# Constant matmuls on TensorE in the first units and before the fp32 job; units through the eleventh's routing ahead of the third job

## The chip, the cores and the metric

The kernel runs on one core of a Trainium2 chip. The metric is the device time of one launch in microseconds (us), as a median of several runs. The engines are named as the profile names them: PE is TensorE (PEld its weight loads), DVE is VectorE, ACT is ScalarE, POOL is GpSimd, SP is SyncE, which here only issues DMAs.

## What is computed

A gated scan over 4 sequences of 3648 tokens of 256 values, and then a mixture of 16 experts in 4 groups of 4. Each token goes to the best group and, in it, to the best expert; its row is multiplied by that expert's two matrices (256 x 1024 and 1024 x 256) and by the two softmax weights.

```python
f = lower_bound + (1.0 - lower_bound) * sigmoid(f_logit);  i = 1.0 - f
for t in range(S):
    h = f[:, t] * h + i[:, t] * x[:, t];  y[:, t] = h
x = y.reshape(B * S, D)                      # 14592 rows of 256
g_idx = argmax(x @ w_group, axis=1)
e_idx = argmax(xg @ w_expert[g], axis=1)     # rows of group g
out[tok_idx] = g_w * e_w * (maximum(x_e @ w1[g, e], 0.0) @ w2[g, e])
```

## The kernel before

**Units.** The 14592 tokens are cut into 29 units of 512. A unit's data is loaded into a tile `zt` by one DMA (line 179). ACT forms the gate (tanh in line 189, an affine step of two pieces in line 199); DVE multiplies (line 215 or 235, one instruction of 1024 columns) and scans (line 226, two instructions of 512 columns into `h`). PE transposes `h` back to rows (line 253, eight 128-column transposes per unit; ACT copies them in line 255) and forms router logits (line 267; ACT copies `rs` in line 270; PE turns them in line 278; ACT copies `Lg` in line 279).

**Routing.** Units are routed in groups, mostly of two. DVE finds the best group and expert (lines 288 to 306), PE counts with the constant matrices `tri`, `upto` and `ones` (lines 313 and 314, in the first nine units lines 368 to 371), DVE makes positions (`both` in line 336 up to `posi` in line 344) and weights (lines 320 to 330). POOL then scatters each block of 128 rows to its expert's list `xs` in HBM (line 348, eight scatters per group of two units).

**Jobs.** Sixteen early jobs, one per expert, each start as soon as a given unit (the cut) has been routed: cut 7 for the first two, 9 for the third and fourth, 11 for the fifth and sixth, and so on. They take 256 rows or more. Sixteen later jobs do the rest. A job's rows `xr` are loaded from `xs` by SP (line 805), and transposed on PE (line 885). Its weights come in four pieces `st` of 512 KB (line 823); ACT makes the upper half `wh` (line 831) and DVE the lower half `wl` (line 832). The first product is three matmuls per block (lines 938 to 940), evicted by ACT as `hh` (line 943) and by DVE as `hl` (line 944); the second product is line 968. One chunk of 256 rows is 48 matmuls of each product. The very first job runs in fp32 without halves (lines 916 and 951); the text calls it the fp32 job. The fourth job is the one that follows the third; "the fifth job's rows" are those of the first job with cut 11.

**Order.** Each engine works strictly through its own list. In the last part of the function a loop goes over the jobs; between their matmuls `bg_step` takes steps from `bgq`, the list of unit and routing steps, at a rate that has them done when a later job is due. `start_macro` first runs `bg_to(marks[cut])`, which empties `bgq` to the point at which the next job's rows are asked for. The program's scheduler then fixes the order on each engine from this sequence, and it can shift instructions against each other. PSUM tiles come from `bank`: three buffers for `m1`, two for `m2`, three for `p`.

Of the kernel before, what the change touches and what calls it, by code (L numbers as in the profile page):

```python
# [18 lines left out]
P = 128  # L19
NE = 16  # L20
UNIT = 512
# [24 lines left out]
def gated_scan_moe(ctx: ExitStack, tc, zx, lower, wroute, wexp, out, S):  # L46
    nc = tc.nc
# [27 lines left out]
    def bank(tag):  # L75
        return ps.tile([P, UNIT], F32, name=f"ps_{tag}", tag=tag, bufs=PS_BUFS[tag])
# [49 lines left out]
    tri = const.tile([P, P], BF16, name="tri")  # L126
    nc.gpsimd.tensor_scalar(out=tri, in0=dmat, scalar1=0.0, scalar2=None, op0=ALU.is_gt)
    upto = const.tile([P, P], BF16, name="upto")
# [109 lines left out]
    def p1_back(u, i):  # L238
# [17 lines left out]
        if i == 0:  # L256
            nc.scalar.copy(rows.bitcast(I32)[:, 0:nt, D], tokno[:, a // P:a // P + nt])

    def p1_router(u):
        a, b = unit_range(u)  # L260
        nt = (b - a) // P
        h = units[u]["h"]
        rp = bank("p")
        for k in range(KD):
            for j in range(nt):
                q = 32 * j
                nc.tensor.matmul(rp[q:q + 32, 0:P], wr[:, k, :], h[:, k, j * P:(j + 1) * P],
                                 start=(k == 0), stop=(k == KD - 1), tile_position=(0, q))
        rs = p1.tile([P, P], F32, name="rs")
        nc.scalar.copy(rs[0:32 * nt], rp[0:32 * nt, 0:P])  # L270
        units[u]["rs"] = rs
# [9 lines left out]
    def route_thunks(G, T, fast=False):  # L281
# [80 lines left out]

        def f4():
            pp = R["pp"] = bank("p")
            oh16 = R["oh16"]
            pv = pp[:, 0:(T + 1) * NE].rearrange("p (t e) -> p t e", e=NE)
            run = state["runoff"][0:1, None, :].broadcast_to([1, T + 1, NE])
            nc.tensor.matmul(pv, row1, run, start=True, stop=False)
            nc.tensor.matmul(pv[:, 0:T], upto, oh16, start=False, stop=False)
            for t in range(T):  # L370
                nc.tensor.matmul(pv[:, t + 1:T + 1], ones, oh16[:, t:t + 1, :].broadcast_to([P, T - t, NE]),
                                 start=False, stop=(t == T - 1))
# [461 lines left out]
    def job_xt(j, pi):  # L834
        b0, rows = j.pieces[pi]
        ch = max(i for i, (a, _) in enumerate(j.chunks) if a <= b0)
        c0 = b0 - j.chunks[ch][0]
        if j.raw:
            j.xh[ch] = mo.tile([P, 2 * P], F32, name="xh", bufs=X_BUFS)
            j.xl[ch] = mo.tile([P, 2 * P], F32, name="xl", bufs=X_BUFS)  # L840
        elif c0 == 0:
            j.xh[ch] = mo.tile([P, KD, 2 * P], F16, name="xh", bufs=X_BUFS)
            j.xl[ch] = mo.tile([P, KD, 2 * P], BF16, name="xl", bufs=X_BUFS)
# [183 lines left out]
    def bg_to(n):  # L1027
        while done[0] < n:
            bg_pop()
# [80 lines left out]
    for mi, mac in enumerate(macros):  # L1110
        if mi < len(PLAN):
            continue
        q = deque()
        if mi + 1 < len(macros):
            start_macro(mi + 1)
            for j in macros[mi + 1]:
                q.extend(prep_thunks(j))
        left = work(mac)
        for j in mac:
            for ch in range(len(j.chunks)):  # L1120
                for cs in j.cols[ch]:
                    m1_step(j, ch, cs)
                    left -= len(cs)
                    bg_step(q, left - 2, len(cs))
                if pending is not None:
                    pj, pc = pending
                    for t in range(len(pj.parts[pc])):
                        m2_step(pj, pc, t)
                        left -= 1
                        bg_step(q, left - 2, 1)  # L1130
                    if pc == len(pj.chunks) - 1:
                        live[0] -= 1
                pending = (j, ch)
        while q:
            q.popleft()()
# [66 lines left out]
```

## Time and profile before

| | us |
|---|---|
| median of three runs (774.38 to 777.86) | 775.78 |
| the profiled execution | 776.59 |
| its span, first to last instruction | 774.8 |
| PE busy in the span | 716.6 (92%) |
| DVE busy | 533.9 (69%) |
| ACT busy | 458.8 (59%) |

Times within the profile count from the span's start; 1.8 us lie outside it. The page gives busy time by engine, the other views used below are tables of stretches (busy time of each engine and the clock that TensorE was granted, 1.00 for 2.4 GHz and 0.50 for 1.2 GHz), lists of who waited for whom, and instructions of one engine in order of time. An entry in square brackets at the end of a row is the idle time before the instruction and what ended it.

### The profile page before, as it was taken

The page shows a single profiled execution, that of the slowest core. Times are in us where ns is not written, and L with a number is a line of the kernel's source. Part 1 is how long each engine was busy: PE and PEld are TensorE (multiplying, and loading weights), DVE is VectorE, ACT ScalarE, POOL GpSimd, SP SyncE. Part 2 cuts the span into 40 slices and gives each one's busy share as a digit, 9 for nine tenths or more (in the row PEclk, how much of TensorE's full clock was granted, in tenths as well). Part 3 has the DMA queues.
Part 4 walks back from the last instruction along what each step waited for, and adds up shares of the span by engine and source line. Part 5 has one row for each costly group of instructions (what it writes and reads, how often), then busy time and mean ns, then how long its engine had stood idle before and what let it go on. Part 6 is the DMA issues. An engine that isn't in the chain of part 4 may idle for free.

```text
span 774.8 us, 20906 instructions
## 1 busy us (share of the span) xinstructions
PE 716.6 (92%) x8055; PEld 633.7 (82%) x8055; DVE 533.9 (69%) x1046; ACT 458.8 (59%) x822; POOL 286.6 (37%) x272
## 2 busy tenths in 40 slices
PE   2656996989999999999999999999999999999995
PEld 1434885778888888889888898999999999999995
DVE  6898798898999976786465545555564676666640
ACT  6586785867878955455455444454555465555541
POOL 3663248276556543642111122213222322232222
PEclk9985998999999999999999999999999999999998
DMA  7998898889998845588656343553553556555300
GB/s 278 352 376 301 306 303 246 320 281 314 317 326 287 266 152 124 171 223 203 170 133 135 120 101 108 134 127 120 139 168 101 158 158 173 158 168 175 88 30 24
DMA packets 104037, 151.75 MB, mean 196 GB/s; under 512 B 63938, under 2 KB 73952, under 8 KB 100608
## 3 DMA queue, kind: packets, MB, share of 16 engines
q1 hardware_dynamic: 89248, 102.00, 45.3%
q0 software_dynamic: 11424, 30.02, 10.8%
q10 hardware_dynamic: 3264, 18.39, 6.9%
q8 instruction: 63, 1.03, 0.6%
q14 instruction: 38, 0.31, 0.1%
HBM read 112.69 MB, written 38.19 MB: 195 GB/s over the span
## 4 chain that ended last, share of the span: by engine, by line
PE 63%; DVE 11%; issue 10%; DMA 10%; POOL 4%; ACT 1%; SPq 0%; POOLq 0%; DVEq 0%; ACTq 0%
PE ps_m L968 29%; PE ps_m L938 7%; PE ps_m L939 7%; PE ps_m L940 7%; DMA xs<-rows,posi 4%; DMA zt<-in_zx_dram 3%; PE ps_p L938 3%; PE ps_p L940 3%; PE ps_p L939 3%; POOL out_dram L981 3%; DVE h L226 2%; DVE wl L832 2%; DMA xr<-xs 2%; PE ps_p L253 1%; DVE hl L944 1%
## 5 line engine op out<-in xcount | busy, mean ns | idle before, releaser
L968 PE MATMUL ps_m<-wh,hl 128*128 128x256 f16 (+4 forms) x1304 | 261.4, 251 | 0.0
L968 PE MATMUL ps_m<-wl,hh 128*128 128x256 bf16 (+4 forms) x1304 | 261.2, 250 | 0.1
L968 PE MATMUL ps_m<-wh,hh 128*128 128x256 f16 (+4 forms) x1304 | 261.1, 251 | 0.0
L968 PEld LDWEIGHTS <-hh 128*128 128x128 f16 (+2 forms) x2608 | 192.3, 99 | 23.4 <-issue 3.7
L938 PE MATMUL ps_m<-xh,wh 128*128 128x256 f16 (+11 forms) x766 | 192.7, 261 | 7.2 <-DVE hl L944 7.2
L939 PE MATMUL ps_m<-xl,wh 128*128 128x256 bf16 (+11 forms) x766 | 192.7, 261 | 0.3 <-DVE xl L895 0.3
L940 PE MATMUL ps_m<-xh,wl 128*128 128x256 f16 (+11 forms) x766 | 192.7, 261 | 0.0
L832 DVE TENSOR_TENSOR wl<-st,wh 128x1024 bf16<-128x1024 f32 x124 | 149.6, 1218 | 55.2 <-ACT wh L831 54.0
L348 POOL DMA_INDIRECT xs<-rows,posi x114 | 135.2, 1186 | 129.3 <-DVE rows L330 47.6
L981 POOL DMA_INDIRECT out_dram<-o,info x75 | 86.2, 1150 | 242.4 <-ACT o L980 221.1
L944 DVE SCALAR_TENSOR_TENSOR hl<-ps_m,hh 128x512 bf16<-128x512 f32 (+9 forms) x172 | 114.5, 668 | 74.5 <-ACT hh L943 73.7
L943 ACT ACTIVATE hh<-ps_m 128x512 f16<-128x512 f32 (+9 forms) x172 | 101.1, 588 | 65.9 <-PE ps_m L940 65.9
L831 ACT CAST wh<-st 128x1024 f16<-128x1024 f32 x124 | 128.2, 1048 | 14.7 <-PE ps_m L968 8.9
L939 PEld LDWEIGHTS <-wh 128*128 128x128 f16 x1072 | 105.4, 98 | 13.8 <-issue 6.3
L938 PEld LDWEIGHTS <-wh 128*128 128x128 f16 x1072 | 105.4, 98 | 10.2 <-issue 2.0
L940 PEld LDWEIGHTS <-wl 128*128 128x128 bf16 x1072 | 105.4, 98 | 8.0 <-issue 0.5
L968 PEld LDWEIGHTS <-hl 128*128 128x128 bf16 (+4 forms) x1304 | 103.0, 99 | 10.1 <-issue 0.2
L981 POOL DMA_INDIRECT out_dram<-o,meta x55 | 60.8, 1105 | 109.6 <-ACT o L980 98.6
L980 ACT ACTIVATE o<-ps_m,info 128x256 f32<-128x256 f32 (+4 forms) x75 | 33.1, 442 | 84.3 <-PE ps_m L968 77.0
L938 PE MATMUL ps_p<-xh,wh 128*128 128x256 f16 (+13 forms) x306 | 73.4, 252 | 0.0
L939 PE MATMUL ps_p<-xl,wh 128*128 128x256 bf16 (+13 forms) x306 | 73.3, 252 | 0.0
L940 PE MATMUL ps_p<-xh,wl 128*128 128x256 f16 (+13 forms) x306 | 73.3, 252 | 0.0
(168 smaller groups left out, 769.8 us busy)
## 6 DMA issues: line engine op xcount, KB each, us to landing
st<-in_wexp_dram SPq DMA_DIRECT2D x124, 512.0 KB, 5.0
zt<-in_zx_dram ACTq DMA_DIRECT2D x17, 1024.0 KB, 9.6
zt<-in_zx_dram SPq DMA_DIRECT2D x9, 1024.0 KB, 8.0
xs<-blank SPq DMA_DIRECT2D x26, 258.0 KB, 6.7
xr<-xs SPq DMA_DIRECT2D x11, 258.0 KB, 4.9
xr<-xs SPq DMA_DIRECT2D x16, 129.0 KB, 3.5
xr<-xs SPq DMA_DIRECT2D x32, 64.0 KB, 2.2
xs<-rows,posi POOLq DMA_INDIRECT x114, 6.0
```

Of the source, the lines that this page charges most:

```text
L226: nc.vector.tensor_tensor_scan(out=h[:, k, c0 - a:c1 - a], data0=ff[:, k, c0 - a:c1 - a], data1=uu[:, k, c0 - a:c1 - a], initial=init, op0 ...
L348: sc = nc.gpsimd.indirect_dma_start(out=xs_v[G["t0"] + t][:, :], out_offset=bass.IndirectOffsetOnAxis(ap=R["posi"][:, t:t + 1], axis=0), i ...
L831: nc.scalar.copy(j.wh[i], j.st[i])
L832: nc.vector.tensor_tensor(out=j.wl[i], in0=j.st[i], in1=j.wh[i], op=ALU.subtract)
L938: nc.tensor.matmul(po, w1_at(j.wh, k, c), xh[:, k], start=(k == 0), stop=False)
L939: nc.tensor.matmul(po, w1_at(j.wh, k, c), xl[:, k], start=False, stop=False)
L940: nc.tensor.matmul(po, w1_at(j.wl, k, c), xh[:, k], start=False, stop=(k == KD - 1))
L943: nc.scalar.activation(hi, pv, AF.Relu)
L944: nc.vector.scalar_tensor_tensor(out=j.hl[ch][:, cs[0]:cs[-1] + 1, 0:w], in0=pv, scalar=0.0, in1=hi, op0=ALU.max, op1=ALU.subtract)
L968: nc.tensor.matmul(pm[i * q:i * q + n, 0:dw], h[ch][:, c, ts], w2_at(w, c)[:, i * dw:(i + 1) * dw], start=(c == 0 and s == 0), stop=(c == ...
L980: nc.scalar.activation(o[s, 0:dw], pm[s, 0:dw], AF.Copy, scale=lt.bitcast(F32)[s, r, 1:2])
L981: nc.gpsimd.indirect_dma_start(out=out_v[out_n[0]].rearrange("n (g d) -> (n g) d", g=g), out_offset=bass.IndirectOffsetOnAxis(ap=lt[s, r, ...
```

## The change

Three additions. A helper `keep_warm` issues n matmuls of 128 columns of two constants into the last quarter of an `m2` bank that nobody reads. It is called with 6 behind the router matmuls of units 2 to 7, with 16 ahead of the counting matmuls of the group of units 7 and 8, and with 22 ahead of the transposes of the fp32 job's rows. And before the third job (`mi == 2`) the unit steps are run through `marks[11]`, the point at which the fifth and sixth jobs' rows are asked for; before, that happened when the fourth job started, with part of the steps spread over the third job.

```diff
+    def keep_warm(pm, n):
+
+        for _ in range(n):
+            nc.tensor.matmul(pm[:, UNIT - P:UNIT], tri, upto, start=True, stop=True)
+
     def p1_router(u):
...
+        if 2 <= u <= EARLY[0][0]:
+            keep_warm(bank("m2"), 6)
         rs = p1.tile([P, P], F32, name="rs")
...
         def f4():
             pp = R["pp"] = bank("p")
+            if G["t0"] * P == EARLY[0][0] * UNIT:
+                keep_warm(bank("m2"), 16)
...
         if j.raw:
+            keep_warm(bank("m2"), 22)
             j.xh[ch] = mo.tile([P, 2 * P], F32, name="xh", bufs=X_BUFS)
...
         if mi < len(PLAN):
             continue
+        if mi == 2:
+            bg_to(marks[11])
         q = deque()
```

The scheduler's order changes with it. On ACT, around the start of the fp32 job (72 us in the trace), two tanh steps (of `zt_797` and `zt_991`) stood together ahead of the row copies:

```order
L199 ACTIVATE zt_759<-zt_759,mid_85,half_83 128x512 x2
L189 ACTIVATE zt_797<-zt_797 128x1024
L189 ACTIVATE zt_991<-zt_991 128x1024
L255 COPY rows_869<-ps_p_870 128x2x256
L257 COPY rows_869<-tokno_102 128x4
L255 COPY rows_869<-ps_p_877 128x2x256
L385 COPY runoff_897<-ps_p_856 128x16
L199 ACTIVATE zt_797<-zt_797,mid_85,half_83 128x512
```

Now the second of them (`zt_1073`, the same unit's tile) comes later, between a logits copy and an eviction of the fp32 job:

```order
L189 ACTIVATE zt_839<-zt_839 128x1024
L255 COPY rows_928<-ps_p_929 128x2x256
L257 COPY rows_928<-tokno_102 128x4
L255 COPY rows_928<-ps_p_936 128x2x256
L394 COPY runoff_956<-ps_p_898 128x16
...
L286 COPY Lg_1123<-ps_p_1124 128x80
L189 ACTIVATE zt_1073<-zt_1073 128x1024
L929 ACTIVATE hl_1058<-ps_m1_1135 128x512
L199 ACTIVATE zt_1073<-zt_1073,mid_85,half_83 128x512 x2
L904 CAST xh_1141<-ps_p_1143 128x512
```

One tanh step has moved back past the row copies, the copy of `runoff` and the two fp32 evictions `hh`.

On DVE, from about 106 us of the trace, the old list had the third job's evictions and the fourth job's weight halves between the steps of the routing of units 11 and 12:

```order
L226 SCALAR_TENSOR_TENSOR h_1270<-zt_1107,h_1109 128x128
L944 SCALAR_TENSOR_TENSOR hl_1362<-ps_m1_1363,hh_1361 128x512
L226 SCALAR_TENSOR_TENSOR h_1270<-zt_1107 128x384
L832 TENSOR_TENSOR wl0_1381<-st_946,wh0_1380 128x1024
L832 TENSOR_TENSOR wl1_1387<-st_948,wh1_1386 128x1024
L288 TENSOR_REDUCE mx_1433<-Lg_1242 128x40
```

In the new one that routing stands in a row, and the same evictions and halves follow it:

```order
L313 SCALAR_TENSOR_TENSOR scn_1482<-rmask8_135,oh16_1480 128x128
L343 TENSOR_TENSOR both_1592<-ps_p_1556,both_1328 128x32
...
L351 TENSOR_REDUCE posi_1597<-sc_1594 128x8
L215 SCALAR_TENSOR_TENSOR zt_1350<-zt_1350 128x1024
L954 SCALAR_TENSOR_TENSOR hl_1526<-ps_m1_1527,hh_1525 128x512
L226 SCALAR_TENSOR_TENSOR h_1455<-zt_1350,h_1352 128x512
L841 TENSOR_TENSOR wl0_1545<-st_1028,wh0_1544 128x1024
L841 TENSOR_TENSOR wl1_1551<-st_1030,wh1_1550 128x1024
L954 SCALAR_TENSOR_TENSOR hl_1526<-ps_m1_1565,hh_1525 128x512
L841 TENSOR_TENSOR wl2_1583<-st_1110,wh2_1582 128x1024
L841 TENSOR_TENSOR wl3_1589<-st_1212,wh3_1588 128x1024
```

What moved is the routing of units 11 and 12, which went ahead of the third job's evictions. From the `both` of the group before (99.95 us in the trace) to the `both` of the group of units 15 and 16 (173.40 us) the two lists hold the same 120 instructions, in another order.

On PE the fourth job's first matmuls stood behind one transpose group and the routing matmuls:

```order
L253 MATMUL ps_p_1495<-ident_76,h_1109 128x128 x4
L938 LDWEIGHTS wh0_1380
L938 MATMUL ps_m1_1627<-xh_1469,wh0_1380 128x256
L313 LDWEIGHTS tri_125
L313 MATMUL ps_p_1542<-scn_1482,tri_125 128x16
```

Now those routing matmuls have gone by, 27 products earlier, and two blocks (`1777`, `1814`) are opened with one matmul each:

```order
L272 MATMUL ps_p_1691<-h_1352,wr_87 32x128 x8
L948 LDWEIGHTS wh0_1544
L948 MATMUL ps_m1_1777<-xh_1631,wh0_1544 128x256
L948 LDWEIGHTS wh0_1544
L948 MATMUL ps_m1_1814<-xh_1631,wh0_1544 128x256
L253 MATMUL ps_p_1735<-ident_76,h_1352 128x128 x4
L285 MATMUL ps_p_1772<-ident_76,rs_1700 128x128
L949 LDWEIGHTS wh0_1544
L949 MATMUL ps_m1_1777<-xl_1632,wh0_1544 128x256
```

The second of these blocks takes the PSUM buffer of the third job's block `1616`, so it stands behind that block's eviction on DVE. On SP the loads of the fifth and sixth jobs' rows now stand ahead of four weight pieces that went before them; on POOL eight scatters of units 11 and 12 now stand ahead of three output writes.

## Rows read from the trace of the kernel before

**Rows 1.** Page, part 1: busy us, share of the span and instructions of PE.

```profile
PE 716.6 (92%) x8055; PEld 633.7 (82%) x8055; DVE 533.9 (69%) x1046; ACT 458.8 (59%) x822; POOL 286.6 (37%) x272
```

**Rows 2.** Stretches: length, busy us of each engine (instructions), clock, DMA share, GB/s.

```profile
core 0: us, PE busy (x) PEld busy (x) DVE busy (x) ACT busy (x) POOL busy (x), PEclk, DMA share, GB/s
73.50:117.00 43.50, 43.41 (x353) 36.38 (x353) 37.45 (x64) 33.62 (x68) 16.70 (x15) 0.93 0.94 315
117.00:134.10 17.10, 10.95 (x83) 7.89 (x81) 14.84 (x29) 11.15 (x20) 14.05 (x11) 0.80 0.82 247
134.10:175.00 40.90, 36.33 (x354) 31.17 (x353) 35.22 (x63) 29.56 (x55) 19.03 (x17) 0.96 0.88 294
175.00:260.00 85.00, 83.49 (x890) 74.10 (x890) 80.15 (x151) 68.31 (x128) 53.06 (x44) 1.00 0.91 311
```

**Rows 3.** Waits of PE, 80 to 190 us: total us, times, longest.

```profile
PE ps_p L885 <- DMA xr<-xs: 5.7, 2, 4.6
PE ps_m L938 <- DVE hl L944: 4.8, 4, 2.1
```

**Rows 4.** Waits of DVE, 80 to 190 us.

```profile
DVE hl L944 <- ACT hh L943: 7.7, 3, 7.0
```

**Rows 5.** DVE in order of time: start us, length us, line, shape, count, idle before.

```profile
74.22 0.16 DVE L568 SCALAR_TENSOR_TENSOR posA<-runoff,taken 128x2 int32<-128x2 f32 x1 [2.22 <-ACT runoff L385]
78.31 2.46 DVE L226 TENSOR_TENSOR_SCAN h<-zt,h 128x512 f32<-128x512 f32 x2
85.16 1.22 DVE L215 SCALAR_TENSOR_TENSOR zt<-zt 128x1024 f32<-128x1024 f32 x1 [4.40 <-ACT zt L199]
...
99.95 0.18 DVE L336 TENSOR_TENSOR both<-ps_p,runoff 128x32 f32<-128x32 f32 x1
115.58 2.35 DVE L832 TENSOR_TENSOR wl<-st,wh 128x1024 bf16<-128x1024 f32 x2
138.88 0.69 DVE L944 SCALAR_TENSOR_TENSOR hl<-ps_m,hh 128x512 bf16<-128x512 f32 x1 [7.04 <-ACT hh L943]
173.40 0.18 DVE L336 TENSOR_TENSOR both<-ps_p,both 128x32 f32<-128x32 f32 x1
```

**Rows 6.** PE in order of time around 99, 117 and 129 us.

```profile
98.88 0.19 PE L313 MATMUL ps_p<-scn,tri 128*128 128x16 bf16 x1
...
116.87 0.19 PE L313 MATMUL ps_p<-scn,tri 128*128 128x16 bf16 x1
...
128.79 1.41 PE L885 MATMUL ps_p<-ident,xr 128*128 128x128 f32 x4 [4.62 <-DMA xr<-xs]
```

**Rows 7.** SP's DMA issues around 126 us.

```profile
126.60 2.70 SPq L805 DMA_DIRECT2D xr<-xs  x4
```

**Rows 8.** Stretch 50 to 55 us, columns as in rows 2.

```profile
50.00:55.00 5.00, 0.69 (x3) 0.51 (x4) 4.97 (x8) 4.30 (x7) 3.78 (x5) 0.72 1.05 399
```

**Rows 9.** PE in order of time, first units to fp32 job.

```profile
46.18 1.95 PE L253 MATMUL ps_p<-ident,h 128*128 128x128 f32 x8
...
49.99 0.33 PE L278 MATMUL ps_p<-ident,rs 128*128 128x128 f32 x1 [0.93 <-ACT rs L270]
...
61.29 0.47 PE L278 MATMUL ps_p<-ident,rs 128*128 128x128 f32 x1 [0.39 <-ACT rs L270]
...
68.34 0.26 PE L369 MATMUL ps_p<-oh16f,upto 128*128 128x128 bf16 x1 [2.18 <-DVE oh16f L359]
...
75.44 1.22 PE L916 MATMUL ps_m<-xh,wh 128*128 128x256 f32 x2
...
80.05 0.70 PE L916 MATMUL ps_m<-xh,wh 128*128 128x256 f32 x2
```

**Rows 10.** Chain that ended last, one piece: start us, length us, what.

```profile
343.83 5.24 PE ps_m L968 x48
```

**Rows 11.** ACT in order of time around the fp32 job's start.

```profile
72.00 1.06 ACT L189 ACTIVATE zt<-zt 128x1024 f32<-128x1024 f32 x1 [1.61 <-DMA zt<-in_zx_dram]
...
74.00 0.18 ACT L385 COPY runoff<-ps_p 128x16 f32<-128x16 f32 x1
...
83.61 1.52 ACT L199 ACTIVATE zt<-zt,mid,half 128x512 f32<-128x512 f32 x2
```

## The prediction

> **What bounds the kernel now.** First the page: PE is busy for 716.6 us of 774.8 [rows 1], so the idle time of PE is what a change of order can give, and only where it stands after PE's dense work begins. The table of stretches says where that is. From 73.5 to 117 us PE is busy 43.41 of 43.5 us; then it loses 17.1 - 10.95 = 6.15 us up to 134.1, 40.9 - 36.33 = 4.6 us up to 175, and 1.5 us in the 85 us after that [rows 2]. The list of waits names two causes: the transposes of a job's rows waited 4.6 us once for their DMA, and first-product matmuls waited 4.8 us in four places for DVE's evictions, which give PSUM buffers back [rows 3]. So I read DVE next. It starts without a pause at 85.16 us, behind a 4.40 us wait for an affine step of ACT [rows 5], and from then to 175 us it is full, but for one hole: 7.04 us ahead of the eviction at 138.88 [rows 5], almost all of its 7.7 us of waiting for `hh` there [rows 4]. The two engines hold each other up in turn: PE stood at 128.79 us for the fifth job's rows [rows 6], which SP could not ask for before 126.60 us [rows 7], when the last scatter of units 9 and 10 had landed; and DVE then ran dry behind PE. The clock adds to it. The rows of 117 to 134.1 us have a clock of 0.80, that is 17.1 x 0.20 / 0.5 = 6.8 us at the lower level, and PE's work after 128.79 us fell into them, at a loss of about (134.1 - 128.8) / 2 = 2.65 us.
>
> So between 85 and 175 us DVE's list sets the pace, and a change there is worth the DVE idle time that it removes; after 175 us PE sets it, and a lead of both engines stays to the end.
>
> **The clock in the first units.** The granted clock falls in the stretch 50 to 55 us, whose mean of 0.72 puts the fall at 50 + (0.72 - 0.5) / 0.5 x 5 = 52.2 us [rows 8]; PE had 0.69 us of work in those 5 us. From the mean of 0.93 in 73.5 to 117 us it rises at 73.5 + 43.5 x 0.07 / 0.5 = 79.6 us [rows 2]. But it is not simply full before 52 us: the logits transpose took 0.33 us at 49.99 and 0.47 us at 61.29 [rows 9], and I take it that PE was at 2.4 GHz only for a short while around 50 us, behind the dense piece of eight transposes at 46.18 [rows 9] and the router matmuls after it. PE's work from 73.6 to 79.6 us lies on the path, since PE is dense from there: at the upper level it would take half, so at most 3 us are to be had here.
>
> **The dummies.** A product of 256 columns at the upper clock takes 5.24 / 48 = 0.109 us [rows 10], so one of 128 columns takes about 0.055 us there and 0.11 us at the lower level. The six in each of units 2 to 7 cost PE 0.66 us at most and stand between the router matmuls and the logits transpose, which waited 0.39 us for ACT anyway [rows 9]: 0.27 us later at the worst, in a stretch that DVE and the input DMAs fill. I cost them at nothing; without that cover it would be 6 x 0.27 = 1.6 us. The sixteen (1.8 us) fit into the 2.18 us that PE waits for `oh16f` at 68.34 [rows 9]. The twenty-two end about 2.4 us after the transposes that follow 68.34, near 73.2 us, where the fp32 job's rows began in the old order: they cost nothing to 0.5 us.
>
> **The start of the fp32 job.** On ACT the second tanh leaves the place ahead of the row copies. It had waited 1.61 us for its input and ran 1.06 us [rows 11], so `runoff`, copied at 74.00 us [rows 11], comes about 2.5 us sooner, and DVE's 2.22 us wait for it [rows 5] goes. The scans at 78.31 [rows 5] then end near 78.5 instead of 80.8 us. That alone is worth nothing, for late next is the affine step at 83.61 us [rows 11] that ended DVE's 4.40 us wait: in the new list the tanh (1.06 us) and an eviction of the fp32 job (0.5 us) stand between the logits copy and it, which makes it 1.55 us later against PE's third group of fp32 matmuls. So DVE's start at 85.16 moves by what PE gains up to there, less 1.55 us. PE gains 1.3 us from its order alone (three transposes have gone ahead of the first fp32 matmuls, and the rows come a little sooner), and up to 3 us from the clock: two fp32 matmul passes start 1.02 us apart at the lower level and 0.53 us apart at the upper one, within the 1.22 and 0.70 us of the rows [rows 9]. If the clock rises no sooner than before, DVE starts 0.2 us later; if it is up when the dummies end, about 3 us sooner. I take 1.5 us. The nearest row is the short logits transpose at 49.99 [rows 9], behind a piece of work less dense than sixteen and twenty-two dummies with eight transposes, and those end at 73 us: the clock should come up somewhere within the fp32 matmuls.
>
> **The units ahead of the third job.** From the `both` at 99.95 to the one at 173.40 us [rows 5] DVE took 73.45 us, and both orders hold the same 120 instructions between these points. Of this it was idle for 7.7 us [rows 4] and work the rest. What the new order leaves idle is the unknown, between nothing and all of it. In the new order PE reaches the second routing product with 28 products and two fp32 rows fewer ahead of it: the old one took 116.87 - 98.88 = 18.0 us without a pause [rows 6, 2], the new one 18.0 - 28 x 0.109 - 0.9 - 0.4 = 13.6 us, which is at 112.5 us; DVE has its part ready at about 111.1 us and waits 1.4 us, with the way through PSUM 1.9 us. At the third product I count 0.7 us more. That is 2.6 us, so DVE saves 7.7 - 2.6 = 5.1 us.
>
> PE pays for it in one place. Its wait at 128.79 us becomes a wait in front of the fourth job: the blocks opened there need buffers and `xl` behind the new DVE piece, two pairs of `wl` (2.35 us each), two gates (1.22), two scans (1.23), four evictions and `xl` (0.6 each, lengths as in [rows 5]) and a dozen small steps, 13.8 us in all, while PE has 27 products and 1.6 us of transposes and router, 4.5 us. So PE waits some 9 us between 117 and 127 us, more than the 6.15 us it lost in the old place, and the clock falls again as it did in the old wait, for about the same 2.65 us. The rows of the fifth job are then there in time: their scatters are not later than before, and PE asks about 2 us later than 128.79. It is returned afterwards: when PE starts the fifth job, DVE has the units' steps behind it, and the 4.6 us that PE lost from 134.1 to 175 us [rows 2] shrink to about 1. The four weight pieces that now queue on SP behind the row loads are issued near 129.5 us instead of 100 to 117 us, and ACT wants the first of them at about 133 us; two or three microseconds of slack, which a load under heavier traffic could eat.
>
> **The sum.** Against the profiled execution: 776.6 - 5.1 - 1.5 = 770.0 us. It stands 0.8 us above the median of the three runs, which I leave out as being within their spread; the forecast for the median is 770.0 us. The bounds: all DVE idle time gone and the clock up early gives 776.6 - 7.7 - 3.0 = 765.9, and 764.5 with the 1.4 us that PE lost to the clock behind 172 us; little saved (2 us) and the clock no sooner gives 776.6 - 2 + 0.2 = 774.8.
>
> **Rivals.** (1) The clock is not raised by the dummies, and the rest works: 776.6 - 5.1 + 0.2 = 771.7 us. For it speaks that PE ran at the lower level from 52.2 to 79.6 us although it was far from idle. The Trainium skill (TensorE: Matmul & The Clock Gate, Part 4: PE-mode transpose) says that transposes do not count towards the upper clock as other matmuls do; by that rule the eight transposes ahead of the dummies bring nothing, and it would be this rival's time. The trace does not bear it out fully, for the short transpose at 49.99 us [rows 9] came behind eight others.
> (2) The stall is only moved. PE's new wait of 9 us is 2.9 us above the old 6.15, and if PE's later waits of 4.6 us stay because DVE, though ahead in units, is still late with evictions, the time is 776.6 + 2.9 - 1.5 = 778 us, or 775 with half of them gone. For it speaks that DVE is full on both sides of the hole; against it, that the same 120 instructions cannot take as long without the hole.
> (3) Slower: the clock. The new wait is longer than those after which it fell. If it then stays low, not for 6.8 us but as long as in the first stretch (79.6 - 52.2 = 27.4 us), because DVE's pace keeps breaking up PE's work, PE loses 13.7 us instead of 2.65, and the time is 770.0 + 11 = 781 us. It decides the sign from a low stretch of some 22 us on.
>
> **Chances.** Forecast 0.52, rival 1 0.16, rival 2 0.20, rival 3 0.12. A measurement of this kernel can tell 0.5% from no change, that is 3.9 us: faster lies below 771.9, slower above 779.7 us. The forecast's case is mostly below 771.9 (0.47 of its 0.52), rival 1 half (0.08), rival 2 within; this gives faster 0.55, same 0.33, slower 0.12. The range of 765.5 to 778 us leaves out rival 3 and the far end of the lower bound.
>
> **What would show it.** In the new profile: DVE starts its full stretch near 83.6 us; the clock is up well before 79.6 us; the hole of 7 us in DVE is gone; PE waits some 9 us in two pieces before the fourth job, for `hl` and `xl`, and not for `xr`; the time between the two `both` falls from 73.4 to about 68 us; after 175 us all is as before, 6 to 7 us sooner. It would be wrong if a DVE hole of several microseconds opens elsewhere, if `wh` casts wait for `st` around 130 us, or if the clock stays low after the new wait.

## The result and the profile after

The changed kernel takes 767.97 us (median of 6 runs, 766.54 to 771.36) against 776.29 us before on the same chip: a ratio of 0.9895 with a 95% interval of 0.9868 to 0.9921, that is 8.3 us. Side by side on another chip (e11 below) it was 772.36 against 779.49 us, 0.9922 (0.9894 to 0.9950). The profiled execution took 766.54 us, the fastest of the six, with a span of 764.8 us; against the profiled execution before that is 10.0 us, and the steps below add up to these 10.0, some 2 us more than the medians show.

The table of stretches of the changed kernel, with the limits and columns of [rows 2]:

```profile
core 0: us, PE busy (x) PEld busy (x) DVE busy (x) ACT busy (x) POOL busy (x), PEclk, DMA share, GB/s
73.50:117.00 43.50, 41.91 (x371) 34.61 (x370) 36.13 (x66) 31.38 (x62) 18.61 (x18) 1.00 0.93 313
117.00:134.10 17.10, 10.70 (x88) 8.74 (x89) 16.83 (x30) 13.39 (x23) 10.53 (x9) 0.80 0.77 253
134.10:175.00 40.90, 40.56 (x423) 35.89 (x421) 40.67 (x74) 36.40 (x68) 25.94 (x20) 1.00 1.01 372
175.00:260.00 85.00, 85.00 (x897) 75.65 (x896) 83.13 (x152) 69.41 (x130) 55.58 (x44) 1.00 0.89 309
```

From 134.1 us on PE hardly stops: 0.34 us idle up to 175 and none up to 260, where it had lost 4.6 and 1.5 us. From 117 to 134.1 us it loses as much as before (6.4 us), at the same mean clock of 0.80; it is another wait. DVE is busy for 40.67 of 40.9 us where it was for 35.22.

DVE in order of time (start, length, line, shape; idle time before and what ended it), to be laid beside [rows 5]:

```profile
83.03 1.23 DVE L215 SCALAR_TENSOR_TENSOR zt<-zt 128x1024 f32<-128x1024 f32 x1 [4.43 <-ACT zt L199]
...
97.80 0.18 DVE L343 TENSOR_TENSOR both<-ps_p,runoff 128x32 f32<-128x32 f32 x1
...
111.16 0.19 DVE L343 TENSOR_TENSOR both<-ps_p,both 128x32 f32<-128x32 f32 x1 [1.84 <-PE ps_p L321]
...
165.84 0.18 DVE L343 TENSOR_TENSOR both<-ps_p,both 128x32 f32<-128x32 f32 x1
```

The full stretch starts 2.13 us sooner (83.03 against 85.16 us), and from `both` to `both` it takes 165.84 - 97.80 = 68.04 us instead of 73.45. DVE's list of waits from 80 to 190 us has three entries left, and no `hh`:

```profile
DVE zt L215 <- ACT zt L199: 4.4, 1, 4.4
DVE both L343 <- PE ps_p L321: 1.8, 1, 1.8
DVE mx L295 <- ACT Lg L286: 0.3, 1, 0.3
```

PE's list of waits for the same stretch (total us, times, longest), beside [rows 3], has lost the 4.6 us for `xr` and gained 5.1 us for ACT's `xh`:

```profile
PE ps_m L948 <- ACT xh L904: 5.1, 1, 5.1
PE ps_m L948 <- DVE hl L954: 2.0, 2, 1.6
PE ps_p L320 <- ACT rows L255: 0.6, 1, 0.6
PE ps_m L949 <- DVE xl L905: 0.3, 1, 0.3
PE ps_p L895 <- DMA xr<-xs: 0.2, 1, 0.2
```

The granted clock in stretches of 2 us rises at 66.0 us, where it had risen at 79.5 us. In this trace that is while the sixteen dummies run (line 262 from 65.14 us), and it stays up although PE then waits 2.08 us for the fp32 job's rows. That the dummies also cause the rise is not shown by this; the table of the clock further down is against it.

```profile
64.00:66.00 2.00, 1.61 (x22) 1.10 (x15) 1.90 (x2) 0.98 (x4) 0.00 (x0) 0.50 1.12 214
66.00:68.00 2.00, 1.06 (x12) 0.83 (x11) 1.83 (x7) 1.75 (x4) 0.00 (x0) 1.00 0.76 274
...
65.14 1.48 PE L262 MATMUL ps_m<-upto,tri 128*128 128x128 bf16 x16
72.96 0.77 PE L895 MATMUL ps_p<-ident,xr 128*128 128x128 f32 x4 [2.08 <-DMA xr<-xs]
```

### The profile page after: what moved, and what is told of

Same layout as the page of the kernel before. It is cut to its first block, busy times and chain, and to the rows that moved or that the text cites. A ratio compares the mean times of both kernels' runs of the same rounds, so it can differ in the third digit from the quotient of the medians.

```text
span 764.8 us, 21052 instructions
## 1 busy us (share of the span) xinstructions
PE 712.4 (93%) x8129; PEld 632.9 (83%) x8129; DVE 534.4 (70%) x1046; ACT 458.3 (60%) x822; POOL 291.5 (38%) x272
## 4 chain that ended last, share of the span: by engine, by line
PE 64%; DMA 14%; DVE 9%; issue 7%; ACT 2%; POOL 2%; SPq 1%; POOLq 0%; ACTq 0%; DVEq 0%
PE ps_m L978 31%; PE ps_m L948 7%; PE ps_m L949 7%; PE ps_m L950 7%; DMA zt<-in_zx_dram 5%; PE ps_p L948 3%; DMA st<-in_wexp_dram 3%; PE ps_p L950 3%; PE ps_p L949 3%; DVE wl L841 3%; DMA xs<-blank 2%; DMA xs<-rows,posi 2%; DVE h L226 2%; POOL out_dram L991 2%; DMA xr<-xs 2%
## 5 line engine op out<-in xcount | busy, mean ns | idle before, releaser
L953 ACT ACTIVATE hh<-ps_m 128x512 f16<-128x512 f32 (+9 forms) x172 | 101.0, 588 | 66.8 <-PE ps_m L950 65.1
L991 POOL DMA_INDIRECT out_dram<-o,meta x55 | 65.1, 1183 | 107.1 <-ACT o L990 94.7
L948 PE MATMUL ps_p<-xh,wh 128*128 128x256 f16 (+13 forms) x306 | 73.3, 252 | 0.0
L949 PE MATMUL ps_p<-xl,wh 128*128 128x256 bf16 (+13 forms) x306 | 73.3, 252 | 0.0
L950 PE MATMUL ps_p<-xh,wl 128*128 128x256 f16 (+13 forms) x306 | 73.3, 252 | 0.0
```

Source lines behind the costliest of these rows:

```text
L948: nc.tensor.matmul(po, w1_at(j.wh, k, c), xh[:, k], start=(k == 0), stop=False)
L949: nc.tensor.matmul(po, w1_at(j.wh, k, c), xl[:, k], start=False, stop=False)
L950: nc.tensor.matmul(po, w1_at(j.wl, k, c), xh[:, k], start=False, stop=(k == KD - 1))
L953: nc.scalar.activation(hi, pv, AF.Relu)
L991: nc.gpsimd.indirect_dma_start(out=out_v[out_n[0]].rearrange("n (g d) -> (n g) d", g=g), out_offset=bass.IndirectOffsetOnAxis(ap=lt[s, r, ...
```

## The experiments

The theory has two terms that add up: the dummies start DVE's full stretch sooner, and the unit steps ahead of the third job take the hole out of DVE. The rivals: one of the two does it all, or the early start is absorbed at a later wait. Each part was run alone, and each of the three groups of dummies was left out.

One thing has to be said first. The runs e1 to e10 fell on two chips on which this program is 5 to 6% slower (the kernel before takes 816 to 827 us there, against 776 and 779 us on the other two) and scatters by 1% from run to run: e1 to e4, e9 and e10 on one, e5 to e8 on the other. The mean granted clock is not the reason (0.94 to 0.99 on the slow two, 0.96 to 0.99 on the others). On these chips the traces hold idle time, the gaps of the text below, that ends with nothing that the profile can name; the last section has what is known of it. No trace of the kernel before was taken there. So every reading below is taken twice: the time against the kernel before on the same chip, and two distances within the trace that leave the gaps ahead of them out. Gaps within them stay: from the logits transpose to DVE's start e9 takes 4.27 us (88.00 to 92.27) where the kernel before took 1.98 (83.18 to 85.16), so the distances of e1 to e10 are compared with each other. They are "to the start": from PE's counting matmul of the group of units 7 and 8 (line 378, first of its row) to the start of DVE's full stretch; and "between": from the first `both` of the full stretch to that of units 15 and 16.

| run | what is in it | us (before) | ratio (95%) | to the start | between | DVE's longest idle time between |
|---|---|---|---|---|---|---|
| before | nothing | 776.29 | 1 | 16.82 | 73.45 | 7.04, for `hh` |
| after | both parts | 767.97 | 0.9895 (0.9868 to 0.9921) | 14.80 | 68.04 | 1.84, for PE |
| e11 | both parts | 772.36 (779.49) | 0.9922 (0.9894 to 0.9950) | 14.23 | 69.31 | 2.14, for PE |
| e12 | both, padded | 770.59 (779.49) | 0.9893 (0.9867 to 0.9920) | 14.52 | 69.03 | 3.02, for PE |
| e1 | units only | 813.06 (816.13) | 0.9981 (0.9950 to 1.0012) | 17.76 | 75.30 | 8.21, cause not shown |
| e5 | units only | 821.58 (827.33) | 0.9945 (0.9897 to 0.9993) | 18.85 | 76.85 | 8.48, cause not shown |
| e9 | units only | 813.80 (816.51) | 0.9966 (0.9923 to 1.0010) | 18.13 | 75.25 | 8.27, cause not shown |
| e2 | dummies only | 813.35 (816.13) | 0.9940 (0.9896 to 0.9985) | 18.28 | 73.96 | 8.12, for `hh` |
| e6 | dummies only | 824.15 (827.33) | 0.9946 (0.9895 to 0.9998) | 15.54 | 75.04 | 8.63, for `hh` |
| e10 | dummies only | 819.18 (816.51) | 1.0065 (1.0025 to 1.0104) | 15.34 | 73.29 | 6.70, for `hh` |
| e3 | without the 16 | 814.73 (816.13) | 0.9979 (0.9939 to 1.0018) | 18.63 | 74.90 | 8.23, cause not shown |
| e7 | without the 16 | 823.13 (827.33) | 0.9942 (0.9905 to 0.9979) | 18.79 | 77.18 | 8.44, cause not shown |
| e4 | without the 22 | 813.53 (816.13) | 0.9958 (0.9918 to 0.9999) | 16.84 | 76.00 | 8.74, cause not shown |
| e8 | without the 6 | 820.53 (827.33) | 0.9849 (0.9750 to 0.9949) | 15.81 | 76.37 | 8.48, cause not shown |

### The unit steps alone: e1, e5, e9

```diff
-        if 2 <= u <= EARLY[0][0]:
+        if False:
             keep_warm(bank("m2"), 6)
...
-            if G["t0"] * P == EARLY[0][0] * UNIT:
+            if False:
                 keep_warm(bank("m2"), 16)
...
-            keep_warm(bank("m2"), 22)
+            pass
```

> Only the unit steps ahead of the third job, no dummies. The list of DVE is that of the changed kernel; on ACT the second tanh stays ahead of the row copies as in the kernel before. Theory (two terms that add up): DVE starts its full stretch at about 85.2 us as before, the time between the two `both` is about 68 us, and the kernel gains its 5.4 us there and some 2.5 us behind it: about 770 us against 776.3 before. Rival A (the early start is absorbed later, the order does all): 768 us, like the changed kernel. Rival B (only an early start lets the new order work): the hole of DVE opens elsewhere, 775 us or more.

> The kernel of e1 once more, on a chip on which the engines are hopefully fed with instructions without gaps as in the first two traces (in e1 engines stood for 4 to 9 us at a time with nothing that they waited for). Theory (two terms that add up): DVE starts its full stretch at about 85.2 us as before, `both` to `both` takes about 68 us, the hole of 7 us is gone, and the time is 6 us below the kernel before. Rival A (the early start is absorbed later): 8 us below, as the changed kernel. Rival B (only an early start lets the new order work): within 2 us of before.

> The kernel of e1 and e5 on a third chip; on the first two, DVE stood 8.2 and 8.5 us ahead of the second `both` with nothing in the trace that it waited for. Theory (those stalls belong to the chips, the terms to the order): where `both` is not held up, DVE starts its full stretch at about 85.2 us, `both` to `both` takes about 68 us and the time is 6 us below before; where it is held up again, `both` to `both` takes 75 us and the time is 2 to 4 us below before. Rival (the new order needs the early start): 75 us between the two `both` without such a stall, and no gain.

DVE's list here is that of the changed kernel, and on ACT the second tanh stands ahead of the row copies as before. The 7 us hole ahead of an `hl` is gone in all three, as the theory says. But on these chips another stands in its place, at the second `both`. DVE of e1, and beside it PE's second routing product, whose result `both` reads and whose row stands 7 us sooner:

```profile
121.12 0.42 DVE L313 TENSOR_TENSOR_SCAN scn<-rmask,oh 128x128 bf16<-128x128 bf16 x1
...
129.75 0.19 DVE L343 TENSOR_TENSOR both<-ps_p,both 128x32 f32<-128x32 f32 x1 [8.21 <-remote]
...
122.38 0.19 PE L321 MATMUL ps_p<-scn,ones 128*128 128x16 bf16 x1
```

Without these 8.2 to 8.5 us, "between" would be 67.0 to 68.4 us; the 1.8 to 3.0 us that after, e11 and e12 wait at the same place belong to it, so 69 to 71 us is the fairer figure against the forecast's 68. With them the order gains nothing between the two `both`, and 2.7 to 5.8 us in the time, with two of three intervals that include 1. "To the start" is 17.8 to 18.9 us: without the dummies nothing starts sooner. (e9 and e10 were to run on a third chip and fell on that of e1 again.)

### The dummies alone: e2, e6, e10

```diff
         if mi == 2:
-            bg_to(marks[11])
+            pass
```

> All the dummies, without the unit steps ahead of the third job. Theory (two terms that add up): clock up near 66 us, DVE's full stretch starts near 83 us, but DVE's hole of some 7 us and PE's wait of 4 to 5 us for the rows of the fifth job are still there, all 2 us sooner: 774 us. Rival A (the early start is absorbed at the wait for the rows): 776 us, as before. Rival B (the dummies do most of it): below 771 us.

> The kernel of e2 once more. Theory (two terms that add up): clock up near 66 us, DVE's full stretch starts 2 us sooner, near 83 us, the hole of 7 to 8 us is still in DVE (e2 had it), `both` to `both` 73.4 us, and the time is 2 us below before. Rival A (absorbed at the wait for the fifth job's rows): the same time as before. Rival B (the dummies do most): 5 us or more below.

> The kernel of e2 and e6 on a third chip. Theory: DVE's full stretch starts 2 us sooner than in the kernel of e9 on the same chip, or more where the engines of the first units stand still for reasons of the chip; the hole of 7 to 9 us ahead of an `hl` is there, `both` to `both` takes 73 to 75 us, and the time is 2 to 4 us below before. Rival (absorbed at the wait for the fifth job's rows): the same time as before.

The hole ahead of an `hl` stands in all three, 6.7 to 8.6 us long, and "between" is 73.3 to 75.0 us: the dummies do nothing for it, as the theory says. "To the start" falls to 15.3 and 15.5 us in two of them. In e2 it does not (18.28), with the same program on the same chip as e10. These are e2 and then e10, each with the transposes of the fp32 job's rows, the logits transpose of the next unit and the clock of the stretch behind the rows:

```profile
76.33 0.83 PE L895 MATMUL ps_p<-ident,xr 128*128 128x128 f32 x4 [1.96 <-DMA xr<-xs]
84.45 0.27 PE L285 MATMUL ps_p<-ident,rs 128*128 128x128 f32 x1
78.00:80.00 2.00, 2.00 (x7) 1.73 (x6) 1.90 (x3) 0.68 (x2) 1.59 (x2) 0.50 1.00 363
...
80.18 0.91 PE L895 MATMUL ps_p<-ident,xr 128*128 128x128 f32 x4 [1.39 <-DMA xr<-xs]
86.75 0.27 PE L285 MATMUL ps_p<-ident,rs 128*128 128x128 f32 x1
82.00:84.00 2.00, 2.00 (x17) 1.36 (x15) 1.90 (x3) 0.89 (x3) 1.39 (x3) 1.00 1.00 373
```

The 2.94 us between the two are not the clock alone. In e2 the clock is at its lower level for 3.4 us (77.4 to 80.8), and from the rows to the logits transpose PE takes 8.12 us instead of 6.57, 1.55 more. Another 0.56 us is the longer wait for the rows, and 0.82 us comes behind the logits transpose, where ACT idles before its affine step (2.03 us in e2, 1.18 in e10). A wait of PE does not decide it: the changed kernel waited longer for the same rows, 2.08 us, and kept the clock. The times don't settle what this part is worth: 0.9940 and 0.9946, and 1.0065 in e10, which was forecast as 2 to 4 us faster and came out 2.7 us slower although its trace has the early start. I have no cause for that.

### One group left out: e3, e7, e4, e8

```diff
-            if G["t0"] * P == EARLY[0][0] * UNIT:
+            if False:
                 keep_warm(bank("m2"), 16)
```

> The changed kernel without the sixteen dummies. On ACT the second tanh then stands ahead of the row copies as in the kernel before, while the other dummies stay; so clock and order of ACT are told apart. Theory (clock): the twenty-two raise the clock by about 73 us without the sixteen; `runoff` comes about 1.5 us later than in the changed kernel, but the affine step now comes right behind the logits copy, so DVE starts its full stretch at about 82 us: 767 us. Rival A (the sixteen are what raises the clock): PE's fp32 products run at 1.2 GHz to about 79 us, DVE starts near 85 us, 770 us. Rival B (the order of ACT is what brings the early start): clock up, and DVE starts near 84.5 us all the same.

> The kernel of e3 once more: without the sixteen, with the second tanh of ACT ahead of the row copies as in the kernel before. In e3 the clock came up within the stretch of 73.5 to 80 us only (0.59). Theory (the clock counts, whatever the order of ACT): the clock rises behind the twenty-two, near 73 to 77 us, and DVE starts its full stretch near 83 us or a little sooner; 8 us below before. Rival (the sixteen are needed, or the place of the tanh): DVE starts at 84.5 us or later; 6 us below before.

Without the sixteen, the scheduler puts the second tanh on ACT back ahead of the row copies, and "to the start" is 18.6 and 18.8 us, as without any dummies. The clock of e7 stays at 0.50 up to 76 us, is up from 77.1 us, while the twenty-two run (75.38 to 77.6 us), and is down again from 80.6 us, before the fp32 products begin at 82.26:

```profile
66.00:74.00 8.00, 5.50 (x43) 4.08 (x41) 7.59 (x16) 4.69 (x10) 1.94 (x2) 0.50 0.71 220
76.00:78.00 2.00, 1.61 (x19) 1.44 (x16) 0.70 (x2) 0.96 (x1) 0.53 (x1) 0.72 1.05 389
78.00:80.00 2.00, 0.91 (x5) 0.69 (x5) 0.71 (x3) 2.00 (x7) 1.43 (x2) 1.00 1.05 416
82.00:84.00 2.00, 2.00 (x6) 1.46 (x5) 1.90 (x3) 0.49 (x2) 1.70 (x2) 0.50 1.03 413
```

So the clock does come up with the twenty-two, as expected, but it does not last to the start of the products, and in e3 it is the same (up 78.9, down 82.3, products from 83.71 us). The early start is gone, as both rivals said. They are not told apart, since clock and order on ACT went away together; and on PE too the transposes and router matmuls around the fp32 job stand in another order than in the changed kernel.

```diff
-            keep_warm(bank("m2"), 22)
+            pass
```

> The changed kernel without the twenty-two dummies. On ACT the second tanh stays in its new place. Theory (the twenty-two hold the clock while PE waits for the fp32 job's rows): the clock rises near 66 us with the sixteen and falls again near 72 us, the fp32 products start at 1.2 GHz, DVE starts near 84.5 to 85 us, 769.5 us. Rival (the sixteen do it alone, the twenty-two are idle work): clock up throughout, DVE at 83 us, 768 us.

Without the twenty-two the tanh stays in its new place (on PE three transposes move back), the clock is up from 70.9 us, before the first of the sixteen (72.11), and falls at 77.7, while PE waits 3.04 us ahead of the rows; the first fp32 products run at 1.2 GHz up to 84.5 us. "To the start" is 16.84 us, between the two levels. That the clock falls without them fits the theory.

```diff
-        if 2 <= u <= EARLY[0][0]:
+        if False:
             keep_warm(bank("m2"), 6)
```

> The changed kernel without the six dummies in units 2 to 7; the order of ACT, DVE and of the rest of PE is the same as in the changed kernel. Theory (they only switch the clock up for a few short stretches ahead of 50 us in which DVE and the input loads set the pace): the same as the changed kernel, 8 us below before, with DVE's start at 83 us; transposes ahead of 50 us run at 1.2 GHz. Rival (the early units gain from the clock): DVE's start 0.5 to 1.5 us later, and so the end.

The orders of ACT, DVE and the rest of PE are those of the changed kernel. "To the start" is 15.81 us against 15.3 and 15.5 with the six; the ratio (four runs, a wide interval) is no worse than that of the changed kernel. They bring nothing that these runs can tell.

The clock of all traces (us in each trace), taken from stretches of 2 us and, where the column has not changed before, from the length of known instructions:

| run | dummies | 16 begin | clock up | down | up again | fp32 products begin |
|---|---|---|---|---|---|---|
| after | all | 65.1 | 66.0 | | | 74.5 |
| e12 | all | 65.7 | 66.7 | | | 74.8 |
| e11 | all | 67.2 | 65.8 | | | 76.4 |
| e10 | all | 72.7 | 70.8 | | | 81.9 |
| e2 | all | 68.4 | 67.1 | 77.4 | 80.8 | 78.4 |
| e6 | all | 71.8 | 71.7 | 75.2 | 78.6 | 81.1 |
| e8 | no 6 | 70.8 | 70.7 | 74.1 | 77.5 | 80.5 |
| e4 | no 22 | 72.1 | 70.9 | 77.7 | 84.5 | 81.9 |
| e3 | no 16 | | 78.9 | 82.3 | 85.7 | 83.7 |
| e7 | no 16 | | 77.1 | 80.6 | 87.4 | 82.3 |
| e5 | none | | some 72.4 | 75.8 | 86.0 | 84.8 |
| e9 | none | | some 69.5 | 72.9 | 83.2 | 81.4 |
| e1 | none | | 89.3 | | | 84.8 |
| before | none | | 79.5 | | | 75.4 |

Two things stand in it that the theory did not have. The clock can come up at this place without any dummy: in e9 the router matmuls of the unit ahead took 0.90 us and the next logits transpose 0.33, against 1.12 and 0.47 us in the kernel before (from 63.40 and 64.91 us), and it was down again when the counting matmul came. And with the sixteen it was up before them, by 1.2 to 1.9 us, in four of eight traces (e11, e10, e2, e4). Three lines of e9:

```profile
69.19 0.90 PE L272 MATMUL ps_p<-h,wr 128*32 128x128 f32 x16
70.57 0.33 PE L285 MATMUL ps_p<-ident,rs 128*128 128x128 f32 x1 [0.48 <-ACT rs L277]
74.14 0.27 PE L378 MATMUL ps_p<-oh16f,upto 128*128 128x128 bf16 x1 [2.80 <-DVE oh16f L366]
```

So what starts the rise is not shown, and it differs between executions of the same list. What the traces do show is the level under the fp32 products: with the sixteen and the twenty-two it is the upper one from the first product on in six traces of seven (not in e2), and with either or both left out in none of seven.

### Both parts, and a padded list: e11, e12

e11 is the changed kernel itself. e12 adds 24 memsets of one column at the start of DVE's list.

```diff
-    onesf = const.tile([P, NE], F32, name="onesf")
+    onesf = const.tile([P, NE], F32, name="onesf"); pad = const.tile([P, 24], F32, name="pad"); [nc.vector.memset(pad[:, k:k + 1], 0.0) for k in range(24)]
```

> The changed kernel itself, beside the kernel before on the kind of chip that e1 to e10 ran on. Theory (two terms that add up, less what the stall at the second `both` takes): from the counting matmul at the unit 7 and 8 group to the start of DVE's full stretch 15.5 us as in e6, e8 and e10 (17.8 to 18.9 us without the dummies), `both` to `both` 75 to 76 us with a stall of some 8.4 us in it, and 6 to 10 us below before, the sum of what the parts gave. Rival (on these chips nothing is left of the change): within 3 us of before.

> The changed kernel with 24 more memsets of one column on DVE at the very start, where DVE waits for its first DMA anyway; everything behind them is in the same order on every engine, but stands 24 instructions further down DVE's list. It asks what the 8.2 to 8.7 us ahead of the second `both` are, which are on no trace of the first chip. Theory (the list itself arrives late, in pieces of a fixed count): the stall no longer stands at the second `both`; it comes about 24 instructions sooner in the program, near the steps that follow the first `both`, and `both` to `both` changes with it. Rival (something that this `both` waits for and the profile does not show): the stall stays at the second `both`, 8 to 9 us long, and the time is that of e11.

These two fell on a chip without the gaps, and there the changed kernel repeats its first result: 7.1 us below before, DVE's start 14.2 us behind the counting matmul, 69.3 us between, no hole of several microseconds (the longest idle times of DVE are 2.14 us for PE and 1.19 us ahead of an `hl`), the same 5.05 and 1.63 us of PE in front of the fourth job. The rival (nothing left) is out for this kind of chip. For the kind on which it was to be tried the changed kernel as a whole was not run; e8, which lacks only the six, comes nearest to it (6.8 us, interval 0.9750 to 0.9949, four runs). e12 is the same kernel within the intervals (0.9893), and since the stall that it was to move does not occur on this chip, it decides nothing.

## Why the prediction was right, and where it was not

The forecast was 770.0 us, the result 767.97, faster as forecast and within the range. The range says little by itself: 765.5 to 778 us holds the 776.3 us of the kernel before as well. Its steps, in the profiled executions:

- **DVE's start.** Forecast 1.5 us sooner (between -0.2 and 3.0), measured 2.13. The sum's parts were right in kind; the clock gave more than was taken for it. These rows, before and then after, divide the 2.13 us, together with the affine step at 83.61 us [rows 11]:

```profile
73.59 1.13 PE L885 MATMUL ps_p<-ident,xr 128*128 128x128 f32 x4 [2.71 <-ACT rows L255]
83.18 0.27 PE L278 MATMUL ps_p<-ident,rs 128*128 128x128 f32 x1
...
79.38 0.27 PE L285 MATMUL ps_p<-ident,rs 128*128 128x128 f32 x1
81.48 1.51 ACT L199 ACTIVATE zt<-zt,mid,half 128x512 f32<-128x512 f32 x2
```

  The fp32 job's rows are transposed 0.63 us sooner (72.96 us), which ACT's new order gives: PE had waited for its row copies. From there to the logits transpose PE takes 6.42 us instead of 9.59, 3.17 less, of which 0.43 is one pair of products that now stands behind it and 2.7 is the clock. And the affine step starts 2.10 us behind that transpose instead of 0.43, so the tanh and the eviction take back 1.67 us. Clock 2.7, order -0.6: by these rows the earlier start is the clock, as the prediction had it (up to 3 us, and 0.2 us later without it). Its picture of how the clock rises was not right: it expected the dummies to bring it up within the fp32 products, and the clock was up 13.5 us sooner than before, ahead of them; e5 and e9 show such a rise without dummies, so what the dummies seem to do is keep it up, or bring it back, until the products begin. As to its time, rival 1 (the clock is not raised) is out: 2.7 us of clock are in the trace. Of the rule that the prediction took from the Trainium skill (TensorE: Matmul & The Clock Gate, Part 4: PE-mode transpose), that transposes do not count towards the upper clock, the runs settle nothing: in e3 and e7 the clock stayed at 0.50 behind the same eight transposes and router matmuls behind which it came up in e5 and e9.
- **The stretch between the two `both`.** Forecast 5.1 us less, measured 5.41. The hole of 7.04 us is gone, and the 2.6 us forecast in its stead (for the routing products of PE) were 1.84 for PE and 0.31 for ACT's `Lg`, 2.15. e2, e6 and e10 show the hole where the units are not moved, e1, e3 to e5, e7 to e9, e11 and e12, where they are, show at most 1.2 us ahead of an `hl` (e11).
- **PE's new wait.** Forecast some 9 us in two pieces in front of the fourth job, for `hl` and `xl`, and the clock falling again for about as long as before. Measured 5.05 + 1.63 + 0.30 us there and 0.36 + 0.61 us ahead of them, 7.95 in all, and the same 0.80 of clock. Half of the step failed in its cause: the long piece waits for `xh`, which ACT makes. I had counted what DVE has to do there and not ACT, whose list runs without a pause from 110.75 to 121.4 us:

```profile
116.09 2.02 ACT L840 CAST wh<-st 128x1024 f16<-128x1024 f32 x2
117.97 1.09 ACT L189 ACTIVATE zt<-zt 128x1024 f32<-128x1024 f32 x1
118.93 0.62 ACT L953 ACTIVATE hh<-ps_m 128x512 f16<-128x512 f32 x1
119.41 1.54 ACT L199 ACTIVATE zt<-zt,mid,half 128x512 f32<-128x512 f32 x2
120.81 0.61 ACT L904 CAST xh<-ps_p 128x512 f16<-128x512 f32 x1
...
121.47 0.37 PE L948 MATMUL ps_m<-xh,wh 128*128 128x256 f16 x1 [5.05 <-ACT xh L904]
```

  The cast stands behind two pairs of `wh`, a tanh and an affine step. It cost nothing more, since DVE, busy for 16.83 of the 17.1 us from 117 to 134.1, set the pace; rival 2 (the stall only moves) fails on the 4.6 us that are gone behind it.
- **The clock after it.** The low stretch is as long as before, 17.1 x 0.20 / 0.5 = 6.8 us. Rival 3 needed much more; its "some 22 us" is high by its own terms, which give (776.6 - 770.0 + 2.65) x 2 = 18.5 us of PE's work.
- **The rows of the fifth job.** SP asks for them at 120.46 us instead of 126.60, and PE waits 0.2 us. The four weight pieces now queue behind them; on ACT one idle time of 2.03 us, at 130.31 us, ended with a piece of `st`, ahead of a tanh, and PE lost nothing by it.
- **Behind 173 us: the mis-sized term.** The sum took the lead of 7.5 us as final, and named only 1.4 us of clock as a bound. The lead grew from 7.56 us at the fourth `both` (173.40 against 165.84 us) to 10.48 us at the sixth (223.71 against 213.23), and was 10.0 at the end. What the kernel before still lost there:

```profile
170.00:172.00 2.00, 0.13 (x1) 0.10 (x1) 2.00 (x4) 1.14 (x3) 1.91 (x1) 0.92 0.74 260
172.00:174.00 2.00, 1.93 (x19) 1.73 (x18) 2.00 (x9) 0.47 (x2) 1.39 (x3) 0.50 0.69 199
174.00:176.00 2.00, 2.00 (x26) 1.99 (x24) 1.73 (x5) 1.57 (x3) 1.70 (x2) 0.73 0.56 219
...
182.54 0.48 PE L885 MATMUL ps_p<-ident,xr 128*128 128x128 f32 x2 [1.11 <-DMA xr<-xs]
```

  The low clock from 171.7 to 175.1 us, in which PE was busy for some 3.1 us (a loss of 1.5), and 1.5 us of idle time up to 260 us, of which 1.11 for a DMA, are both absent after: the clock is 1.00 from 134.1 to 260 us and PE idles 0.34 us. The first had followed a wait of 2.09 us for DVE's `hl` (at 171.87 us), which is gone too; that the wait for the DMA also came of DVE's lateness is likely and not shown. The forecast knew both numbers: it kept the clock as a bound (1.4 us) and left the other 1.5 us as they were.

So 2.13 + 5.41 + 2.94 - 0.48 = 10.0 us (the last is what the lead loses again behind 325 us, where it was still 10.5) in the profiled executions, of which the medians show 8.3 and, on the second chip, 7.1 us. What stays open is the share of each part in the time on a chip without the gaps: the parts alone never ran on one. On the slow chips their times do not add up to a sum (units 2.7 to 5.8 us, dummies 3 us faster twice and 2.7 slower once), so that the two terms add up, and that the early start is not absorbed at a later wait, is read from the traces and not from the times.

## What to carry to other kernels

When two engines hold each other up in turn, price a change of order by the idle time of the one whose list is otherwise full, and then go through every later wait and every low stretch of the clock that follows from its lateness: the lead takes them back as well. When work is drawn together on one engine, go through the lists of all engines at the place where the next one will wait; here ACT, which no term of the sum had counted, held PE up longest. Dummy matmuls are worth trying where a dense piece of PE work follows a thin one: here they had to stand in both gaps ahead of the piece, up to its start, and even then one trace of seven began the piece at the lower clock. In units that other engines pace nothing was seen of them. And a rise that stands beside the dummies in one trace is not yet their work; look at the same place in a trace without them.

## What the runs showed of the hardware

**Idle time without a shown cause.** On two chips the kernel before takes 816 to 827 us instead of 776 to 779, with the same granted clock. A trace of it was not taken there; e1's span is 38.1 us longer than that of the kernel before on the first chip, with PE 12.2 us longer busy and 25.9 us longer idle. In the list of waits PE has 26 us that the profile puts down to "issue", that is, to nothing that it shows, and none in before and after. The largest entries of e1 (us in total, times, longest; the last from 80 to 190 us):

```profile
PE ps_m L978 <- issue: 12.2, 22, 1.1
PE ps_p L285 <- issue: 9.8, 2, 9.4
DVE hl L954 <- issue: 53.9, 19, 5.6
DVE both L343 <- remote: 8.2, 1, 8.2
```

Such a label is no proof that an engine had nothing to wait for. DVE's 53.9 us ahead of `hl` are mostly waits for `hh` under another name: before had 115.5 us in 92 waits for `hh` there, e1 has 67.6 us in 74 and these 19. The traces of these chips lack part of the semaphore records by which a wait is named; of 608 instructions by which PE signals, e1 has the signal of 557, before 606 of 607.

The seven traces there with the moved units all have 8.2 to 8.7 us ahead of the second `both`, the three without them have none there. The semaphore records, which none of the views lists, say what ended it: in e1 PE's signal for the routing product at 122.38 us came at 129.73 us, 0.02 us before `both` began, and in the other six too the last signal of PE came 0.02 to 0.03 us before it, 4 to 8 us behind the row of the product. In after, e11 and e12 it came 0.2 us behind the row. So DVE was ready and waited for PE's signal; why that was late is not shown. This is against the theory of e12, in which DVE's own list arrives late. The Trainium skill (Runtime: NRT & Kernel Launch, Instruction fetch mechanics) says that each engine streams its list in blocks through a DMA queue of its own and that this is mostly hidden; no run here shows that a list was late, on PE or elsewhere, and e12 ran where the 8 us don't occur.

**The clock column ahead of its first change.** In the trace of before it reads 1.00 up to 52 us, but eight transposes took 1.95 us at 46.18 [rows 9], exactly as long as in the changed kernel at 45.68 us, whose column reads 0.50 there:

```profile
46.00:48.00 2.00, 2.00 (x13) 1.73 (x12) 1.83 (x8) 1.43 (x4) 1.60 (x2) 1.00 1.03 413
...
46.00:48.00 2.00, 2.00 (x16) 1.43 (x14) 1.91 (x6) 1.34 (x4) 1.39 (x3) 0.50 1.03 411
45.68 1.95 PE L253 MATMUL ps_p<-ident,h 128*128 128x128 f32 x8
```

At the upper level the eight take 1.07 to 1.08 us (68.58 us of the changed kernel). A column that has not yet changed in a trace is not a reading; the length of a known instruction is.
